# Eight of the sixteen transfers of turned blocks go from GpSimd's queue to ScalarE's

## The chip, the cores and the metric

The kernel runs on one core of one Trainium2 chip. A core has five engines with a queue of instructions each: PE (TensorE, matmuls), DVE (VectorE), ACT (ScalarE), POOL (GpSimd) and SP (SyncE). Each queue runs in order: an instruction that waits holds back everything behind it on its engine. DMA transfers are issued from the queues of SP, ACT and POOL and then run on 16 DMA engines that all the queues share. The metric is device time in microseconds, the median of several executions. The traces are of one profiled execution each.

## The reference

The input `x` has 8 images of 4096 tokens with 192 channels. A causal convolution with 7 taps comes first (softmax of `weight`, one set of taps for each of 8 heads of 24 channels), then a mixer over tokens, then one over channels:

```python
out = np.einsum('hk,bskhg->bshg', softmax(weight), x_unf)   # 7 taps, causal
xt = x.transpose(0, 2, 1)                                   # x is the result above
h = np.maximum(xt @ w_tok1, 0.0) @ w_tok2                   # 4096 -> 256 -> 4096
u = x + h.transpose(0, 2, 1)
h2 = np.maximum(u @ w_ch1, 0.0) @ w_ch2                     # 192 -> 1536 -> 192
return (u + h2).astype(np.float32)
```

## The kernel before

The images go in five groups: one, one, and three pairs. A group is computed in two stages. The first (convolution on ACT and DVE, lines 646 to 660, and the first token product on PE, lines 762 to 768) runs in the background, woven into the second stage of the group before it. The second stage takes 8 tiles of 512 tokens of the group. A tile goes through these steps:

- **mix2** (lines 921 to 950, or `mix2_halves`, lines 956 to 973, in the last two groups) is the second token product. DVE adds it to the convolved input, which gives `u` (tokens along the partitions), and turns `u` in blocks of 32 by 32 (`nc.vector.transpose`, lines 939, 950 and 973).
- **blocks_sent** (line 995) moves the turned blocks to their places, so that channels stand along the partitions. It is 16 DMA transfers of 48 KB each, all inside the core's SBUF. Until the last one has landed the tile can't be used.
- **parted** (line 1031; `parted_single` for a group of one image) splits the result into a high part (`own_hi`, ACT, line 1042 or 1021) and a low part (`own_lo`, DVE, line 1044 or 1027), and copies halves across partitions for the second image (ACT line 1047, POOL's queue line 1049).
- **channel1** (lines 1080 to 1122) multiplies by `w_ch1`, in six steps of two PSUM tiles. ACT takes the ReLU of each tile into `hh` (line 1121), DVE the rest into `hl` (line 1122), and only then is the PSUM tile free. The pool `ps_x` has six such tiles, so a step can begin when the step three before it has been read by both.
- **channel2** (lines 1156 to 1163, or `channel2_halves`, lines 1139 to 1147) multiplies by `w_ch2`, adds `u`, and stores to `out`.

The order of every queue is written out by the program before it runs (a planner, `Background`, places the background's steps by estimated times; it is not touched here). There are 27 calls of `blocks_sent`. The first three prepare tiles of a group of one image; the next 13 prepare pairs, with background work still running; the last 11 are in the stretch where no background is left. In those last 11, `blocks_sent` is called between the two images of a tile: behind channel1 of the first image and ahead of channel1 of the second. Below the calls are numbered 0 to 26 in order of time.

Each DMA takes one of 16 completion semaphores in turn: eight, named DMAHW0 to DMAHW7, serve the transfers of SP and ACT, and eight, DMASW0 to DMASW7, those of POOL. A transfer waits until the one that last used its semaphore has landed.

The background's split for the first token product is ACT's cast at line 746 (`xhl`, high part) and DVE's subtraction at line 750 (low part); PE's lines 766 to 768 read both.

Of the kernel before, what the change touches and what calls it, by code (L numbers as in the profile page):

```python
# [139 lines left out]
def conv_mixer_kernel(ctx: ExitStack, tc: tile.TileContext, x, weight, w_tok1, w_tok2, w_ch1, w_ch2, out):  # L140
    nc = tc.nc
# [25 lines left out]
    def f32(ap):  # L167
        return ap.bitcast(F32)
# [809 lines left out]
    def own_tile(n):  # L978
        return up.tile([P, ND, TT], F32R, name=f"own_{n}")
# [15 lines left out]
    def blocks_sent(z, nb, pool, name):  # L995

        if nb == 1:
            other = own_tile("lo")  # L1000
            blocks = z[:, :D // QB].rearrange("p (c n) t -> p n c t", n=NQ // 2)
            home = other
        else:
            other = pool.tile([P, 2, ND, TT], F32R, name=name)
            blocks = z.rearrange("p (c n) t -> p n c t", n=NQ)
            home = other[:, 1]
        for k in range(NQ):
            for q in range(NQ):
                i = (q + k) % NQ
                queue = nc.gpsimd if q % 2 else nc.sync  # L1010
                queue.dma_start(
                    out=f32(home[q * QB:(q + 1) * QB, :, i * P:(i + 1) * P]),
                    in_=blocks[i * QB:(i + 1) * QB, q % (2 * nb)],
                )
        return other
# [260 lines left out]
    for gi, bs in enumerate(GROUPS):  # L1276
# [13 lines left out]
        for q in range(NT):  # L1290
            nxt = (gi, q + 1) if q + 1 < NT else (gi + 1, 0)
            for i, b in enumerate(bs):
# [24 lines left out]
                if ready:  # L1317
                    abc = parted(other)
                elif turn:
                    if gi == 0 and nxt[0] == 0:  # L1320
                        bg.require(("t2", nxt[1] // 2, nxt[1] % 2))
                    z = up.tile([P, ND * NQ, P], F32, name="own_hi") if by_blocks else None
                    mix2(*nxt, *loaded, turned=z)
                    mixed[0] = nxt[1]
                    if by_blocks:
                        other = blocks_sent(z, len(GROUPS[nxt[0]]), sp, "other")
                        bg.release()
# [3 lines left out]
                if early:  # L1331
                    z = cps[0].tile([P, RB + HALO, 2, D // 2], F32, name="raw0")
                    z = z.rearrange("p r b d -> p (r b d)")[:, :ND * NQ * P].rearrange("p (n t) -> p n t", t=P)
                    for j in range(TJ):
                        mix2_halves(nxt[0], *loaded, z, j)
                        channel2_halves(i, h, u, osb, [j])
                    spare = not spare
                    other = blocks_sent(z, 2, cps[0] if spare else sp, "xc0" if spare else "other")
                elif ahead:
                    product2(i, h, u, osb, half[0])  # L1340
# [60 lines left out]
```

## Time and profile before

| What | Value |
|---|---|
| median of 3 runs | 2024.13 us (2024.07 to 2025.25) |
| the profiled execution | 2022.08 us |
| its span, first to last instruction | 2020.3 us |
| PE busy | 2010.3 us (100% of the span) |
| DVE busy | 1513.3 us (75%) |
| ACT busy | 756.7 us (37%) |
| POOL busy | 233.9 us (12%) |
| TensorE clock granted | 1.000 |

Views of the profile used below are the page of the profiled execution, the waits by engine, the busy time by windows, the view of one source line, and the timeline. In the timeline a row gives the start (us from the start of the span), the length (us), the engine, the line, the operation, what it writes and reads, and how many instructions were merged into the row. In brackets stands the idle time of the engine before it and what ended it. Engines named SPq or POOLq stand for their sequencers.

### The profile page before, as it was taken

The page shows a single profiled execution, that of the slowest core. Times are in us where ns is not written, and L with a number is a line of the kernel's source. Part 1 is how long each engine was busy: PE and PEld are TensorE (multiplying, and loading weights), DVE is VectorE, ACT ScalarE, POOL GpSimd, SP SyncE. Part 2 cuts the span into 40 slices and gives each one's busy share as a digit, 9 for nine tenths or more (in the row PEclk, how much of TensorE's full clock was granted, in tenths as well). Part 3 has the DMA queues.
Part 4 walks back from the last instruction along what each step waited for, and adds up shares of the span by engine and source line. Part 5 has one row for each costly group of instructions (what it writes and reads, how often), then busy time and mean ns, then how long its engine had stood idle before and what let it go on. Part 6 is the DMA issues. An engine that isn't in the chain of part 4 may idle for free.

```text
span 2020.3 us, 44927 instructions
## 1 busy us (share of the span) xinstructions
PE 2010.3 (100%) x18719; PEld 1860.6 (92%) x18719; DVE 1513.3 (75%) x3021; ACT 756.7 (37%) x1293; POOL 233.9 (12%) x407
## 2 busy tenths in 40 slices
PE   9999999999999999999999999999999999999999
PEld 9789999999999999999999999999999999999998
DVE  8799998999759999757975689556666666666664
ACT  4575544444333434324333334233233222333322
POOL 0100000101221011100111110111111110011110
PEclk9999999999999999999999999999999999999999
DMA  9845346456354577424654434533223222233310
GB/s 308 300 154 177 114 156 202 143 169 200 121 157 132 165 195 204 119 74 123 171 162 115 115 105 134 150 87 85 75 71 83 71 75 58 77 85 85 85 49 17
DMA packets 289626, 260.94 MB, mean 129 GB/s; under 512 B 205520, under 2 KB 238544, under 8 KB 289424
## 3 DMA queue, kind: packets, MB, share of 16 engines
q1 hardware_dynamic: 264736, 169.18, 29.6%
q0 software_dynamic: 24688, 88.89, 14.4%
q8 instruction: 148, 2.42, 0.5%
q14 instruction: 54, 0.44, 0.1%
HBM read 146.60 MB, written 71.30 MB: 108 GB/s over the span
## 4 chain that ended last, share of the span: by engine, by line
PE 95%; DVE 3%; ACT 1%; DMA 1%; issue 0%; POOL 0%; DVEq 0%; POOLq 0%; SPq 0%; ACTq 0%
PE ps_x L1080 38%; PE ps_x L1139 24%; PE ps_x L1156 13%; PE ps_x L1157 6%; PE ps_x L964 2%; PE ps_a L766 2%; PE ps_a L767 2%; PE ps_a L768 2%; PE ps_a L452 1%; PE ps_x L923 1%; PE ps_x L926 1%; PE ps_x L928 1%; PE ps_x L927 1%; DVE xc L659 1%; PE ps_a L762 1%; PE ps_x L989 1%
## 5 line engine op out<-in xcount | busy, mean ns | idle before, releaser
L1121 ACT ACTIVATE hh<-ps_x 128x512 fp32r<-128x512 f32 x756 | 410.7, 596 | 863.2 <-PE ps_x L1080 863.0
L1122 DVE SCALAR_TENSOR_TENSOR hl<-ps_x,hh 128x512 fp32r<-128x512 f32 x756 | 484.4, 685 | 184.1 <-ACT hh L1121 182.6
L1139 PE MATMUL ps_x<-w,hh 64*128 64x384 f32 x3360 | 481.5, 355 | 0.0
L1139 PE MATMUL ps_x<-w,hl 64*128 64x192 f32 x3360 | 423.0, 247 | 0.0
L659 DVE SCALAR_TENSOR_TENSOR xc<-raw,cw,xc 128x384 f32<-128x384 f32 (+1 forms) x768 | 389.0, 561 | 7.6 <-ACT xc L657 7.6
L1156 PE MATMUL ps_x<-w,hh 128*128 128x384 f32 x1344 | 387.2, 360 | 0.1
L1080 PE MATMUL ps_x<-other,w_hi 64*128 64x512 f32 x1296 | 336.8, 388 | 0.0
L1157 PE MATMUL ps_x<-w,hl 128*128 128x192 f32 x1344 | 336.4, 250 | 0.0
L1080 PE MATMUL ps_x<-own_hi,w_hi 64*128 64x512 f32 x1440 | 331.7, 392 | 1.6 <-DVE hl L1122 0.9
L1139 PEld LDWEIGHTS ps_x<-w,hl 64*128 64x128 f32 x3360 | 325.8, 188 | 1.2 <-DVE hl L1122 0.3
L1080 PE MATMUL ps_x<-own_lo,w_hi 64*128 64x512 f32 x1440 | 325.6, 387 | 0.0
L1080 PE MATMUL ps_x<-own_hi,w_lo 64*128 64x512 f32 x1440 | 325.6, 387 | 0.0
L1139 PEld LDWEIGHTS ps_x<-w,hh 64*128 64x128 f32 x3360 | 320.2, 184 | 0.9
L1157 PEld LDWEIGHTS ps_x<-w,hl 128*128 128x128 f32 x1344 | 256.6, 191 | 0.0
L1080 PEld LDWEIGHTS ps_x<-other,w_hi 64*128 64x128 f32 x1296 | 235.7, 184 | 21.6
L1156 PEld LDWEIGHTS ps_x<-w,hh 128*128 128x128 f32 x1344 | 252.4, 188 | 0.7 <-DVE hl L1122 0.7
L1080 PEld LDWEIGHTS ps_x<-own_hi,w_hi 64*128 64x128 f32 x1440 | 210.1, 184 | 34.3 <-issue 4.1
L1080 PEld LDWEIGHTS ps_x<-own_hi,w_lo 64*128 64x128 f32 x1440 | 215.6, 184 | 27.8 <-DVE w_lo L212 0.5
L1080 PEld LDWEIGHTS ps_x<-own_lo,w_hi 64*128 64x128 f32 x1440 | 215.9, 184 | 27.1
L1080 PE MATMUL ps_x<-other,w_lo 64*128 64x512 f32 x648 | 181.5, 386 | 0.0
L1147 DVE TENSOR_TENSOR osb<-ps_x,osb 128x192 f32<-128x192 f32 x420 | 150.2, 358 | 24.3
L1145 DVE TENSOR_TENSOR osb<-ps_x,u 128x192 f32<-128x192 f32 x140 | 49.8, 356 | 136.2 <-PE ps_x L1139 135.6
(165 smaller groups left out, 2443.3 us busy)
## 6 DMA issues: line engine op xcount, KB each, us to landing
raw<-in_x_dram SPq DMA_DIRECT2D x56, 672.0 KB, 7.3
t<-t2d SPq DMA_DIRECT2D x64, 512.0 KB, 5.5
out_dram<-osb POOLq DMA_DIRECT2D x63, 384.0 KB, 4.5
u<-xcd SPq DMA_DIRECT2D x62, 384.0 KB, 5.9
xcd<-xc POOLq DMA_DIRECT2D x28, 768.0 KB, 8.1
t<-t1p SPq DMA_DIRECT2D x32, 512.0 KB, 5.8
t2d<-stage SPq DMA_DIRECT2D x16, 512.0 KB, 3.7
t<-t1d SPq DMA_DIRECT2D x29, 256.0 KB, 5.2
```

The lines of the kernel that those rows point to most:

```text
L659: nc.vector.scalar_tensor_tensor(out=dst, in0=src, scalar=cw[:, h, k:k + 1], in1=dst, op0=ALU.mult, op1=ALU.add)
L766: nc.tensor.matmul(out=ps, lhsT=wh, rhs=xh, start=a, stop=False)
L767: nc.tensor.matmul(out=ps, lhsT=wh, rhs=xl, start=False, stop=False)
L768: nc.tensor.matmul(out=ps, lhsT=wl, rhs=xh, start=False, stop=z)
L1080: nc.tensor.matmul(out=ps, lhsT=w1[w][rows, c, p * P:(p + 1) * P], rhs=t[h][v][rows, c], start=n == 0, stop=n == len(prods) - 1,)
L1121: nc.scalar.activation(out=h["hh", f], in_=ps, func=AF.Relu)
L1122: nc.vector.scalar_tensor_tensor(out=h["hl", f], in0=ps, scalar=0.0, in1=f32(h["hh", f]), op0=ALU.max, op1=ALU.subtract)
L1139: nc.tensor.matmul(out=ps[:, :m], lhsT=h[part, f][ks, ts], rhs=w2[ks, f, :m], start=n == 0 and part == "hh", stop=z and part == "hl",)
L1145: nc.vector.tensor_tensor(out=rows(osb[:, j]), in0=rows(pss[0][:, :D]), in1=tokens(u, i)[:, j], op=ALU.add)
L1147: nc.vector.tensor_tensor(out=osb[:, j], in0=v, in1=osb[:, j], op=ALU.add)
L1156: nc.tensor.matmul(out=ps[:, :2 * D], lhsT=h["hh", f][:, ts], rhs=w2[:, f, :], start=n == 0, stop=False)
L1157: nc.tensor.matmul(out=ps[:, :D], lhsT=h["hl", f][:, ts], rhs=w2[:, f, :D], start=False, stop=z)
```

## The change

In `blocks_sent`, the transfers with odd `q` are put on ScalarE's queue where they were on GpSimd's. The other eight stay on SP's. Sizes, sources, destinations and the order in the program are the same.

```diff
@@ -1007,7 +1007,7 @@
         for k in range(NQ):
             for q in range(NQ):
                 i = (q + k) % NQ
-                queue = nc.gpsimd if q % 2 else nc.sync
+                queue = nc.scalar if q % 2 else nc.sync
                 queue.dma_start(
                     out=f32(home[q * QB:(q + 1) * QB, :, i * P:(i + 1) * P]),
                     in_=blocks[i * QB:(i + 1) * QB, q % (2 * nb)],
```

The order of PE and DVE is unchanged. ACT's queue gains 27 times eight transfers, and POOL's loses them.

The first place is ACT's queue in the last stretch, at call 17 (`raw_17298` is the buffer of turned blocks, `hh_17147` to `hh_17151` are outputs of channel1 for the first image, `hh_17601` and later for the second). Before:

```order
L1121 ACTIVATE hh_17149<-ps_x 128x512 [waits PE_49] x4
L1121 ACTIVATE hh_17151<-ps_x 128x512 [waits PE_49] x4
L1121 ACTIVATE hh_17601<-ps_x 128x512 [waits DVE_49,PE_49]
L1121 ACTIVATE hh_17601<-ps_x 128x512 [waits PE_49] x3
L1121 ACTIVATE hh_17603<-ps_x 128x512 [waits DVE_49,PE_49]
```

The same place in the changed kernel:

```order
L1121 ACTIVATE hh_17151<-ps_x 128x512 [waits PE_49] x4
L1011 DMA other<-raw_17298 32x3x128 [waits DMASW4_49,DVE_49]
L1011 DMA other<-raw_17298 32x3x128
L1011 DMA other<-raw_17298 32x3x128 [waits DMAHW6_49]
L1011 DMA other<-raw_17298 32x3x128 [waits DMAHW0_49]
L1011 DMA other<-raw_17298 32x3x128 [waits DMAHW2_49]
L1011 DMA other<-raw_17298 32x3x128 [waits DMAHW4_49]
L1011 DMA other<-raw_17298 32x3x128 [waits DMAHW6_49]
L1011 DMA other<-raw_17298 32x3x128 [waits DMAHW0_49]
L1121 ACTIVATE hh_17601<-ps_x 128x512 [waits PE_49,Activation_49]
```

The eight transfers stand between the ReLUs of the two images, and the first of them waits for DVE's last turn. The waits on DMAHW semaphores are new too: sixteen transfers share eight semaphores now and take them in turn, so SP and ACT have four each, and each of the last four here waits until the one four before it has landed.

The second place is ACT's queue at call 13, where the background's casts (`xhl`) and the first tap of the next convolution (line 657) follow:

```order
 L1121 ACTIVATE hh_14309<-ps_x 128x512 x4
 L1121 ACTIVATE hh_14311<-ps_x 128x512 x4
+L1011 DMA other<-own_hi 32x3x128 x8
 L746 CAST xhl<-xc_11786 128x768 x2
 L657 ACTIVATE xc_14648<-raw_14177,cw 128x16x24 x4
```

Both casts stand behind the transfers now.

The third is POOL's queue at the same call, where the store of a convolved block (`xcd`, line 694) follows:

```order
 L1170 DMA out_dram<-osb 128x768 x2
-L1011 DMA other<-own_hi 32x3x128 x8
 L694 DMA xcd_79<-xc_13815 128x8x192 x2
 L1049 DMA other<-own_hi 64x1536
 L1049 DMA other<-own_lo 64x1536
```

The store no longer has the transfers, and their wait for DVE, in front of it.

## The prediction

> **What bounds the kernel now.** I read the page first, then the busy time by windows, then PE's waits.
>
> ```profile
> PE 2010.3 (100%) x18719; PEld 1860.6 (92%) x18719; DVE 1513.3 (75%) x3021; ACT 756.7 (37%) x1293; POOL 233.9 (12%) x407
> PE 95%; DVE 3%; ACT 1%; DMA 1%; issue 0%; POOL 0%; DVEq 0%; POOLq 0%; SPq 0%; ACTq 0%
> ```
>
> PE is busy throughout and is 95% of the chain that ended last. The windows (columns: stretch, its length, then busy time and instructions of PE, PEld, DVE, ACT, POOL, the clock, DMA share, GB/s) say it stage by stage:
>
> ```profile
> 1080.00:1377.00 297.00, 297.00 (x2701) 275.75 (x2701) 204.47 (x393) 102.52 (x165) 33.72 (x59) 1.00 0.42 118
> 1377.00:1960.00 583.00, 583.00 (x6736) 538.37 (x6734) 366.11 (x740) 186.21 (x309) 71.83 (x131) 1.00 0.30 77
> ```
>
> In neither stretch does PE idle by 10 ns, and the granted clock is 1.00. Of PE's waits only one, of 1.4 us near the start, is longer than this one:
>
> ```profile
> PE ps_x L1080 <- DVE hl L1122: 0.9, 1, 0.9
> ```
>
> So nothing that makes the transfers land sooner can shorten these stretches: no wait of PE ends with them. The change can only cost time, and it does where ACT, which was free, is now held so long that PE has to wait for it. What counts is how long ACT is held, and how late it may be.
>
> **What it removes and adds.** The view of line 1011 gives the price of one issue (shortest, median, longest in ns); the last row is SP's timeline:
>
> ```profile
> L1011 SPq DMA_DIRECT2D other<-own_hi x104: 585/597/1542, 591.8 to 1335.8; - x104
> L1011 POOL DMA_DIRECT2D other<-own_hi x104: 548/548/582, 592.3 to 1337.3; - x104
> DMA to landing us min/median/max: 1.8/2.1/5.5
> ...
> 1263.21 0.33 SPq L724 DMA_DIRECT2D t<-t1p  x1
> ```
>
> POOL loses 27 x 8 x 548 ns = 118 us of work, which is worth nothing, since POOL is busy for 12% of the span. ACT gains 216 issues. No row shows a DMA issued by ACT. The nearest row is SP's, the same transfers from another engine that isn't POOL: 597 ns. Another transfer of SP's (line 724) was issued in 0.33 us, and the longest of line 1011 here took 1.54; these bound the price, and I take SP's own. Eight in a row are read from the timeline, at call 17, the second of the last stretch:
>
> ```profile
> 1432.56 0.58 DVE L973 STREAM_TRANSPOSE raw<-u 128x384 f32<-128x384 f32 x1
> 1433.27 5.10 SPq L1011 DMA_DIRECT2D other<-raw  x8
> 1436.34 1.09 ACT L1121 ACTIVATE hh<-ps_x 128x512 fp32r<-128x512 f32 x2 [18.87 <-PE ps_x L1080]
> 1436.97 1.29 DVE L1122 SCALAR_TENSOR_TENSOR hl<-ps_x,hh 128x512 fp32r<-128x512 f32 x2 [1.09 <-ACT hh L1121]
> 1440.22 0.39 PE L1080 MATMUL ps_x<-xc,w_hi 64*128 64x512 f32 x1
> ```
>
> **The last stretch, 11 calls.** ACT has been idle for 18.87 us when the second image's channel1 gives it its first ReLU at 1436.34. In the changed kernel its eight transfers start when SP's do, at 1433.27, behind DVE's last turn (1432.56 + 0.58 = 1433.14), and they stand ahead of that ReLU. ACT would be held until 1433.27 + 5.10 = 1438.37: the ReLU is 2.03 us late. Behind it wait `hl` on DVE and then PE, whose fourth step reuses the two PSUM tiles of the first. That step begins at 1440.22, and `hl` had read them by 1436.97 + 1.29 = 1438.26. The spare time is 1.96 us. So ACT may be held for 1436.34 - 1433.27 + 1.96 = 5.03 us from the start of its transfers; each us above that is a us of PE's. Later steps catch up, since ACT needs 1.09 and DVE 1.29 us of a step of about 2.04 us. The undisturbed eight thus cost 0.07 us a call. But not all were undisturbed:
>
> ```profile
> 1377.11 5.97 SPq L1011 DMA_DIRECT2D xc<-raw  x8
> 1657.48 5.83 SPq L1011 DMA_DIRECT2D other<-raw  x8
> 1713.54 5.65 SPq L1011 DMA_DIRECT2D xc<-raw  x8
> 1769.60 6.35 SPq L1011 DMA_DIRECT2D other<-raw  x8
> 1825.64 6.04 SPq L1011 DMA_DIRECT2D xc<-raw  x8
> ```
>
> These five of the eleven took 29.84 us in sum, 4.7 us above five times 5.03. I expect about as many disturbed calls after the change, not the same ones. The semaphores add little of their own: a queue has four, so its fifth transfer comes 4 x 5.10 / 8 = 2.55 us behind its first, and a landing takes 2.1; only slow landings hold the queue, and those are what stretched the five. Term: 4.7 + 6 x 0.07 = 5.1 us. At 0.33 us an issue it is nothing. At 0.75 us (8 x 0.75 = 6.0 us) it is 11 x 0.97 + 4.7 = 15.4 us.
>
> **The casts of the background, calls 5 to 8 and 12 to 15.** ACT had done both casts before the transfers began; now they come behind them. At call 13, and one call later for SP:
>
> ```profile
> 1198.48 0.84 ACT L746 CAST xhl<-xc 128x768 fp32r<-128x768 f32 x1 [2.28 <-PE ps_a L768]
> 1201.82 5.11 SPq L1011 DMA_DIRECT2D other<-own_hi  x8
> 1204.62 0.95 DVE L750 TENSOR_TENSOR xhl<-xc,xhl 128x768 fp32r<-128x768 f32 x1
> 1209.44 0.36 PE L766 MATMUL ps_a<-xhl,t 128*128 128x384 f32 x1
> 1266.55 5.63 SPq L1011 DMA_DIRECT2D other<-own_hi  x8
> ```
>
> From the start of the transfers to PE's first use are 1209.44 - 1201.82 = 7.62 us. A cast (0.84) and a subtraction (0.95) have to follow the transfers, so ACT may be held 5.83 us, some 5.7 with a hand-over between engines (ACT's first ReLU above ended at 1436.34 + 0.60 and DVE started at 1436.97, so 0.03 to 0.05 each). Undisturbed, 0.6 us is left; at call 14, with 5.63, hardly any. What is late next is DVE's work behind line 750, by about 3.5 us, which the idle time on DVE (25% of the span) takes up before the next channel1.
>
> Two of these calls, 7 and 13, get a store in their way:
>
> ```profile
> 1194.96 1.14 DVE L659 SCALAR_TENSOR_TENSOR xc<-raw,cw,xc 128x384 f32<-128x384 f32 x2
> 1202.48 4.36 POOL L1011 DMA_DIRECT2D other<-own_hi  x8 [19.05 <-DMA t<-t1p]
> 1206.83 1.82 POOL L694 DMA_DIRECT2D xcd<-xc  x2
> xcd<-xc POOLq DMA_DIRECT2D x28, 768.0 KB, 8.1
> ```
>
> The convolved block was done at 1194.96 + 1.14 = 1196.10, yet its store (two DMAs, 8.1 us to landing) went behind POOL's transfers at 1206.83. Now it can go at 1196.1, and its second half is still moving when the sixteen transfers start at 1201.82. I price this by the five stretched rows: 0.5 to 1.2 us longer than 5.1, so 0 to 0.5 us over what is left, and take 0.5 us for each of the two. Below it is nothing; above, if each of the two waves of landings took the 5.5 us of the slowest in place of 2.1, some 6 us a call. Term: 1.0 us.
>
> **The other calls, 0 to 4 and 9 to 11.** At call 0 casts and a first tap move behind the transfers too, and the split starts about 1.3 us later. PE's need is here:
>
> ```profile
> 494.92 1.89 DVE L1027 TENSOR_TENSOR own_lo<-own_lo,own_hi 128x512 fp32r<-128x512 f32 x3 [0.75 <-ACT own_hi L1021]
> 498.21 0.50 PE L1080 MATMUL ps_x<-own_hi,w_hi 64*128 64x512 f32 x2
> ```
>
> DVE was done at 496.81, PE began at 498.21, and the low part is used last in a step, so the 1.40 us and more cover it. Without that cover it would be some tenths of a us a call. I cost these calls at nothing.
>
> **The sum.** 5.1 + 1.0 = 6.1 us on the profiled execution of 2022.08 us (its span is 2020.3, so 1.8 us lie around it): 2028.2. The median shown is 2024.13, which is 2.05 us above the profiled execution; with that the forecast is 2030.2, rounded 2030 us.
>
> **Rivals.** (a) *Not slower.* ACT's hold stays under 5.03 us and PE notices nothing. It speaks for it that six of the eleven rows are only 0.07 us above that point, and that POOL needed 4.36 us for the same eight. With POOL's pace the undisturbed calls cost nothing and the five stretched ones, each 0.74 us shorter, 1.2 us in all; the casts have 1.4 us to spare. Time: 2024.13 + 1.2 = 2025.3, which counts as no change. Against it stands that SP, the nearer row, shows no issue under 585 ns. [...]
>
> (b) *ACT issues more dearly than SP,* because its sequencer is slower at it, or because two queues that issue at once share what makes the descriptors. The trace shows SP and POOL side by side, never two queues of this kind, so it can't exclude it; that single issues of SP stretched to 1.54 us says that an issue can be held by something else. At 0.75 us: 15.4 + about 3 for the casts = 18 us, 2042. At twice SP's price, eight take 10.2 us: 11 x 5.2 + 6 x 4.5 + 2 x 3.4 = 91 us, 2115; calls 5 and 6 have a PE use about 1.1 us later. [...]
>
> (c) *Faster:* a POOL that is free earlier, or transfers that land sooner. PE's 583.00 busy us of 583.00 leave no room for either. Time: 2024.
>
> (d) *The change doesn't do what it says:* the order shows it 27 times on ACT, so no chance is kept for it.
>
> **How the numbers follow.** Forecast 0.50, (a) 0.28, (b) 0.19, (c) 0.03. About 0.2%, 4 us, is what a measurement of this kernel can tell from no change. Slower by more than that: 0.50 + 0.19 = 0.69; the same 0.28; faster 0.03. The range goes from 2023, nothing lost and 1 us for the spread of the runs, to 2048: (b) at 0.8 us an issue, 6.4 us held, is 11 x 1.37 + 4.7 + 8 x 0.5 = 24 us. The doubled price lies outside.
>
> **What would show it.** ACT's rows of line 1011 at about 600 ns, eight in 5.1 to 6.4 us. In the last stretch the first ReLU behind them 2 to 3.3 us later, and PE waiting for `hl` of line 1122 at the fourth step of channel1, 0 to 1.3 us a call, some 5 us in all. At the calls with casts, line 750 late by about 4 us and PE's wait at line 766 under 1 us. POOL's `xcd` stores at calls 7 and 13 about 8 to 10 us earlier. I am wrong if an issue on ACT is far from 0.6 us, if PE waits in the last stretch for something other than `hl`, or if most of the loss lies before 1377 us.

## The result: 35 us slower, and the profile after

| | before | changed |
|---|---|---|
| median of 4 runs each | 2024.38 us (2024.07 to 2025.25) | 2059.05 us (2055.71 to 2060.12) |
| ratio | | 1.0168 (95% interval 1.0150 to 1.0185) |
| the profiled execution, its span | 2022.08 us, 2020.3 us | 2057.99 us, 2056.0 us |

The sign is as forecast, the size is not: 35 us where 6 were predicted, outside the range of 2023 to 2048. Engines and chain of the changed kernel, from its page:

```profile
PE 2029.0 (99%) x18719; PEld 1869.5 (91%) x18719; DVE 1508.8 (73%) x3021; ACT 753.7 (37%) x1293; POOL 114.5 (6%) x191
PE 77%; DVE 13%; DMA 3%; ACTq 3%; ACT 2%; issue 1%; SPq 0%; DVEq 0%; POOL 0%; POOLq 0%
```

PE had 95% of the chain and has 77% now; DVE, ACT's sequencer and DMA have the rest. PE's three longest waits (total us, times, longest):

```profile
PE ps_x L1080 <- DVE hl L1122: 8.6, 8, 1.5
PE ps_a L766 <- ACT xhl L746: 4.6, 3, 2.0
PE ps_a L767 <- DVE xhl L750: 1.5, 3, 0.6
```

The view of line 1011 gives the price of one issue on ACT (shortest, median, longest in ns) and the landings:

```profile
L1011 ACTq DMA_DIRECT2D other<-own_hi x104: 592/612/2013, 593.7 to 1355.0; - x104
...
L1011 ACTq DMA_DIRECT2D other<-raw x40: 592/620/1712, 1454.4 to 1919.7; - x40
...
DMA to landing us min/median/max: 1.9/2.0/6.4
```

The waits are the predicted ones: `hl` in the last stretch, the casts at lines 766 and 767 before it. The issue price is the predicted one too, 612 to 620 ns. To see where the time went, compare the intervals between the starts of the calls. For the ten intervals of the last stretch the windows are, before and after (length, then busy PE, PEld, DVE, ACT, POOL):

```profile
1377.11:1937.76 560.65, 560.65 (x6486) 518.14 (x6484) 352.19 (x712) 175.30 (x292) 65.83 (x120) 1.00 0.30 77
```

```profile
1396.27:1971.44 575.17, 568.25 (x6484) 524.37 (x6482) 349.41 (x712) 173.22 (x292) 21.94 (x40) 1.00 0.29 75
```

The same matmuls take 14.5 us longer; the eleventh call adds 2.0 us behind the last of these starts (2056.0 - 1971.44 = 84.6 us to the end, 82.5 before). The other 19.2 us (1396.27 - 1377.11) arose before call 16. So the loss is in two halves of 16.5 and 19.2 us.

**The last stretch.** Some of ACT's eleven batches, from its timeline, then call 17 on each engine:

```profile
1396.27 7.04 ACTq L1011 DMA_DIRECT2D xc<-raw  x8
1454.44 7.29 ACTq L1011 DMA_DIRECT2D other<-raw  x8
...
1685.15 5.66 ACTq L1011 DMA_DIRECT2D other<-raw  x8
...
1971.44 6.72 ACTq L1011 DMA_DIRECT2D xc<-raw  x8
...
1457.45 0.55 POOL L1170 DMA_DIRECT2D out_dram<-osb  x1 [29.59 <-DVE osb L1147]
1461.83 3.05 ACT L1121 ACTIVATE hh<-ps_x 128x512 fp32r<-128x512 f32 x6 [23.24 <-DMA other<-raw]
1462.46 3.68 DVE L1122 SCALAR_TENSOR_TENSOR hl<-ps_x,hh 128x512 fp32r<-128x512 f32 x6 [5.32 <-ACT hh L1121]
1463.21 0.50 PE L1080 MATMUL ps_x<-xc,w_hi 64*128 64x512 f32 x1 [1.48 <-DVE hl L1122]
```

The chain of call 17 reads as predicted: eight transfers, then the ReLU, then `hl`, then PE. But all eleven batches are stretched, to 5.66 to 7.29 us, 70.5 us in sum, where the forecast had five stretched and 60.4 in sum. New is the POOL row. Before the change the same store of the output stood behind POOL's transfers:

```profile
1433.78 4.36 POOL L1011 DMA_DIRECT2D other<-raw  x8 [27.18 <-DVE raw L973]
1438.13 0.59 POOL L1170 DMA_DIRECT2D out_dram<-osb  x1
```

That is 4.86 us after the start of call 17 at 1433.27, when SP's eight were nearly issued. Now it goes 3.01 us after the start at 1454.44, in the middle of the batch, and in all eleven calls alike. The store isn't all of it, though: in call 17 an issue of ACT that began before the store took 1.71 us instead of 0.61. What else stretches batches stands in the section on the stores that are held back.

```profile
1456.40 1.71 ACTq L1011 DMA_DIRECT2D other<-raw  x1
```

Issues like this one are most of the stretch. An undisturbed batch takes 5.16 us (eight issues of 0.61 and seven gaps of 0.04). What the eleven batches take beyond that is 13.7 us: 12.8 lie in single issues of 0.7 to 1.9 us, and only 0.9 in longer gaps, where the waits for the landing of the transfer four before would show. SP's disturbed batches before the change are alike, with one long issue each (1.16 to 1.86 us) and no such gap. At call 23 before:

```profile
1771.52 1.86 SPq L1011 DMA_DIRECT2D other<-raw  x1
```

**The first part.** Six of its intervals hold the whole loss: behind call 0 (32.55 us before, 36.27 now), 5 (64.72, 66.96), 6 (66.09, 68.00), 7 (63.53, 67.73), 13 (64.73, 68.79) and 14 (64.73, 68.49), 19.9 us in sum; the others, each between -1.2 and +1.4 us, cancel. They are of two kinds. At 7, 13 and 14 POOL's store of the convolved block went ahead. Call 7 in the timeline:

```profile
842.08 1.79 POOL L694 DMA_DIRECT2D xcd<-xc  x2 [16.14 <-DVE xc L659]
845.01 8.80 ACTq L1011 DMA_DIRECT2D other<-own_hi  x8
853.86 1.56 ACT L746 CAST xhl<-xc 128x768 fp32r<-128x768 f32 x2 [18.94 <-DMA other<-own_hi]
854.72 0.96 DVE L750 TENSOR_TENSOR xhl<-xc,xhl 128x768 fp32r<-128x768 f32 x1 [7.99 <-ACT xhl L746]
```

And the windows of 3.41 us around the end of PE's wait (length, busy PE, PEld, DVE, ACT, POOL, then the clock, DMA share and GB/s):

```profile
851.49:854.90 3.41, 1.44 (x11) 1.21 (x9) 0.18 (x1) 1.04 (x2) 0.00 (x0) 1.00 0.46 109
854.90:858.31 3.41, 2.99 (x9) 2.60 (x10) 3.38 (x6) 3.16 (x5) 0.55 (x1) 0.50 0.04 8
```

ACT was held 8.80 us (8.33 and 8.12 in calls 13 and 14). In these three calls the waits for landings do hold the queue: the fifth transfer begins 0.9, 2.1 and 1.0 us late, right when the first has landed; the rest is in long issues. Behind PE's wait came 3.41 us at a granted clock of 0.50: PE's matmuls of lines 766 to 768 start 0.32 us apart there, and 0.17 us right behind it. PE was busy for 2.99 us of it, so that about 1.5 us were lost, by my estimate. Half clock followed calls 13 and 14 too, with PE busy for 3.41 and 3.27 us, about 1.7 and 1.6 us lost. At 0, 5 and 6 the batch is ordinary or a little stretched (5.59, 6.65, 5.18 us), but DVE has no idle time left. Behind call 5 it is busy for all of the 12 us from 734.00, behind call 6 for 9.96 of the 10 us from 793.00. Call 0 in the timeline:

```profile
486.49 5.59 ACTq L1011 DMA_DIRECT2D own_lo<-own_hi  x8
492.18 0.62 ACT L730 CAST t<-t 128x512 fp32r<-128x512 f32 x1 [13.77 <-DMA own_lo<-own_hi]
492.83 0.69 DVE L734 TENSOR_TENSOR t<-t 128x512 fp32r<-128x512 f32 x1 [4.68 <-ACT t L730]
```

And what follows it by windows:

```profile
498.20:510.00 11.80, 11.23 (x85) 8.00 (x83) 11.73 (x24) 4.55 (x9) 1.09 (x2) 1.00 0.36 114
```

DVE waits 4.68 us for ACT's cast of `t`, which stands behind the transfers now, and is then busy for 11.73 of 11.80 us. It can't make up what it lost, and PE pays.

### The profile page after: what moved, and what is told of

Its sections match the earlier page's. It is cut to its first block, busy times and chain, and to the rows that moved or that the text cites. A ratio compares the mean times of both kernels' runs of the same rounds, so it can differ in the third digit from the quotient of the medians.

```text
span 2056.0 us, 44524 instructions
## 1 busy us (share of the span) xinstructions
PE 2029.0 (99%) x18719; PEld 1869.5 (91%) x18719; DVE 1508.8 (73%) x3021; ACT 753.7 (37%) x1293; POOL 114.5 (6%) x191
## 3 DMA queue, kind: packets, MB, share of 16 engines
q8 instruction: 148, 2.42, 0.5%
## 4 chain that ended last, share of the span: by engine, by line
PE 77%; DVE 13%; DMA 3%; ACTq 3%; ACT 2%; issue 1%; SPq 0%; DVEq 0%; POOL 0%; POOLq 0%
PE ps_x L1080 30%; PE ps_x L1139 19%; PE ps_x L1156 10%; PE ps_x L1157 4%; DVE xc L659 4%; DVE hl L1122 3%; ACTq L1011 3%; PE ps_x L964 2%; PE ps_a L767 1%; PE ps_a L768 1%; PE ps_a L766 1%; DMA other<-own_hi 1%; DVE osb L1147 1%; PE ps_a L452 1%; PE ps_x L923 1%
## 5 line engine op out<-in xcount | busy, mean ns | idle before, releaser
L1139 PE MATMUL ps_x<-w,hh 64*128 64x384 f32 x3360 | 493.9, 355 | 0.0
L1139 PE MATMUL ps_x<-w,hl 64*128 64x192 f32 x3360 | 473.8, 247 | 0.0
L1139 PEld LDWEIGHTS ps_x<-w,hl 64*128 64x128 f32 x3360 | 392.7, 188 | 0.5
L1139 PEld LDWEIGHTS ps_x<-w,hh 64*128 64x128 f32 x3360 | 391.3, 184 | 0.8
L1080 PE MATMUL ps_x<-other,w_hi 64*128 64x512 f32 x1296 | 341.4, 390 | 5.4 <-DVE hl L1122 4.4
L1080 PE MATMUL ps_x<-own_hi,w_hi 64*128 64x512 f32 x1440 | 336.6, 395 | 4.6 <-DVE hl L1122 2.1
```

Of the source, the lines that this page charges most:

```text
L1080: nc.tensor.matmul(out=ps, lhsT=w1[w][rows, c, p * P:(p + 1) * P], rhs=t[h][v][rows, c], start=n == 0, stop=n == len(prods) - 1,)
L1139: nc.tensor.matmul(out=ps[:, :m], lhsT=h[part, f][ks, ts], rhs=w2[ks, f, :m], start=n == 0 and part == "hh", stop=z and part == "hl",)
```

## Theories

Theory 1, formed from this: ACT's hold is what costs, 1 us for each us above 5.03 in the last stretch, and the hold grew because POOL's stores, no longer queued behind POOL's transfers, collide with the batch. The rivals: two queues that issue side by side and share eight semaphores slow each other by themselves; slow landings cost by themselves, whoever issues; the loss is spread over all calls rather than bound to places.

The experiments, e1 to e12, were run in three groups, each beside the kernel before on the same chip (medians 2023.3, 2022.0 and 2023.1 us in the three). "Ratio" is always to that.

## Experiment: four transfers on ACT instead of eight

```diff
-                queue = nc.scalar if q % 2 else nc.sync
+                queue = (nc.sync, nc.scalar, nc.sync, nc.gpsimd)[q]
```

> Of the eight transfers on ScalarE's queue four go back to GpSimd's (q = 3), and SP keeps eight. Theory 1 (the price is what ScalarE is held above 5.03 us in a call): ScalarE is held about 2.5 us, at most 4 with slow landings, under the 5.03 us, so that the last stretch loses nothing and the casts come 1.9 us earlier than they are needed: 2024 to 2030, mid 2026. Theory 2 (any use of ScalarE's queue next to SP's costs, by contention on the way): about half of the loss of 35 us stays, near 2041.

e2: 2024.37 us, ratio 1.0008 (0.9998 to 1.0017). The ten intervals of the last stretch by windows:

```profile
1379.13:1939.66 560.53, 560.53 (x6484) 518.02 (x6482) 350.88 (x712) 175.28 (x292) 44.20 (x80) 1.00 0.29 77
```

Two of ACT's batches in the timeline, a usual one and the longest:

```profile
1771.50 2.56 ACTq L1011 DMA_DIRECT2D other<-raw  x4
1827.56 4.00 ACTq L1011 DMA_DIRECT2D xc<-raw  x4
```

PE is busy for every one of the 560.53 us. The batch of 4.00 us is stretched (its last issue took 2.04 us, beside landings of 4 to 5 us), as those of the changed kernel are, and costs nothing, because it ends before 5.03 us. So it is the hold, with its threshold, and not the use of ACT's queue as such.

## Experiment: the last eleven calls alone, and the first sixteen alone

`calls` is a list that grows by one with each call of `blocks_sent`, here and in the experiments below.

```diff
-                queue = nc.scalar if q % 2 else nc.sync
+                odd = nc.scalar if len(calls) > 16 else nc.gpsimd      # e3; e4 with the two exchanged
+                queue = odd if q % 2 else nc.sync
```

> ScalarE's queue is used in the last eleven calls only; the first sixteen use GpSimd's, as before. Theory 1 (the loss of each call stands for itself): the eleven intervals lose 14 to 15 us and the tail 2, so 2024.4 + 16.6 = 2041 (2038 to 2044). Theory 2 (the last stretch inherits lateness from the first, in ScalarE's or DVE's queue): clearly less than 16 us, under 2035.

> The other half of the test: ScalarE's queue in the first sixteen calls only, GpSimd's in the last eleven. Theory 1: 2024.4 + 19 = 2043.5 (2040 to 2047), with the half clock behind calls 7, 13 and 14, and the two halves add to the 35 us of the whole. Theory 2 (the halves interact): the sum of the two losses is over 5 us off 35.

e3: 2036.98 us, ratio 1.0069 (1.0054 to 1.0084). e4: 2039.74 us, ratio 1.0075 (1.0058 to 1.0092). By the ratios that is 14.0 and 15.2 us, 29 in sum, against 34 for the whole, at the edge of the 5 us that theory 2 was given; the profiled executions add up better (14.1 and 19.1 of 35.7 us of span). Both are somewhat under what was expected, and e4's runs spread over 4.7 us. The traces show that the last stretch doesn't inherit its loss: in e4, which lost 19 us ahead of it, the ten intervals take 560.64 us, against 560.65 before the change, and in e3 they lose 13.1 us with nothing lost ahead of them.

## Experiment: transfers in the last eleven calls issued between the ReLUs

```diff
+                if q % 2 and len(calls) > 16:
+                    behind.append(send)
+                else:
+                    send()
...
+            for send in [behind.pop(0) for _ in behind[:2 if p < 2 else 1]]:
+                send()
```

> GpSimd's queue in the first sixteen calls; in the last eleven ScalarE issues its eight transfers behind the ReLUs of the six steps of channel1 (two, two, one, one, one, one), so that no ReLU stands behind more than two. Theory 1 (only the hold of ScalarE's queue costs): two issues hold ScalarE 1.2 us, less than the 5.03 us less what a step needs, and the transfers have 30 us until they are needed: 2024 to 2027. Theory 2 (the queue or its traffic costs, wherever the transfers stand): as e3_last11, 2035 or more.

e7: 2023.30 us, ratio 1.0003 (0.9993 to 1.0012). The same eight transfers from the same queue in the same eleven calls, with POOL's stores as free as in e3, cost 14 us in e3 and nothing here. Where they stand in ACT's queue is what counts.

## Experiment: all sixteen on SP

```diff
-                queue = nc.scalar if q % 2 else nc.sync
+                queue = nc.sync
```

> All sixteen transfers on SP, in about 10.5 us; ScalarE has none, and GpSimd's stores are as free as in the changed kernel. Theory 1 (the collision costs only through ScalarE's hold): the last eleven intervals stay at 56.05 us in spite of slow landings, since the moved tile is needed some 30 us later; the calls of the background lose where the landing is late (some 5 us later than before): 2024 to 2035. Theory 2 (slow landings cost by themselves): the last eleven intervals are over 56.5 us as well, 2040 or more.

e8: 2084.87 us, ratio 1.0304 (1.0289 to 1.0319): the total is a miss by 50 us, the part on the last stretch a hit. One batch in SP's timeline:

```profile
1664.94 10.67 SPq L1011 DMA_DIRECT2D xc<-raw  x16
```

The ten intervals by windows:

```profile
1440.62:2001.26 560.64, 560.64 (x6486) 518.13 (x6484) 351.23 (x712) 175.17 (x292) 21.87 (x40) 1.00 0.29 77
```

With POOL's stores free and landings of 3 to 4.6 us among the batches, PE still loses nothing in the last stretch, so slow landings alone do no harm there. In the first sixteen calls the landing, 5 us later, is itself on the path; 63.5 us had been lost by call 16. PE's waits there are for the split of the moved tile:

```profile
PE ps_x L1080 <- ACT other L1047: 11.1, 6, 2.0
PE ps_x L1080 <- ACT own_hi L1021: 7.0, 2, 5.3
```

Theory 1 had taken the background calls to have that much time to spare. They haven't.

## Experiment: POOL's stores held back again

A small read of every moved block on POOL, behind each call, so that no store can start before the transfers have landed. The first version had its scratch in a new tile of 16 bytes a partition, the second in a tile that is dead by then.

```diff
+    gate = const.tile([P, TT // P], F32, name="gate")                                  # e1 only
...
+        nc.gpsimd.tensor_copy(out=gate, in_=f32(home[:, 0, 0:TT:P]))                   # e1
+        nc.gpsimd.tensor_copy(out=csm[:, 0:TT // P], in_=f32(home[:, 0, 0:TT:P]))      # e5
```

> ScalarE keeps its eight transfers. GpSimd reads a column of every moved block behind each call, so that its stores (of the convolved block, line 694, and of the output, line 1170) can't start before the transfers have landed. Theory 1 (GpSimd's stores, freed by the change, collide with the batch): ScalarE's batches fall from a mean of 6.4 us in the last eleven calls to about 5.5; the three batches of 8.7 to 9.1 us (calls 7, 13, 14) fall under 6.5; no stretch of half clock behind them; the eleven intervals lose 8 to 10 us in all over the kernel before, where the changed kernel loses 14.5; total 2036 to 2046, mid 2041. Theory 2 (two queues of the same kind that issue side by side and share eight completion semaphores slow each other, whatever GpSimd does): batches stay at 5.7 to 7.3 us and the time at 2055 or more.

e1: 2058.97 us, ratio 1.0177 (1.0162 to 1.0193): by the total, theory 2. But the trace showed short batches, 5.16 to 5.36 us, in five of the last eleven calls and in calls 13 and 14, and no stretch of half clock; the time was lost elsewhere, in slower matmuls. Hence the second version:

> The same gate on GpSimd, but its scratch is the dead tile csm, so that no buffer moves in SBUF. In e1_gate the batches were short as theory 1 said (5.16 to 5.19 us in calls 13, 14, 19 to 21 and 23, no half clock), yet the matmuls of channel1 came every 0.233 us in place of 0.227 us, from before the first gated call on. Theory 1 (moved buffers made those matmuls slower and hid the gain): pitch 0.227 us again; what is left is some 9 us in the last eleven calls, from batches that other traffic stretches, and some 10 us in the first sixteen, where only calls 7, 13 and 14 gain: 2042 (2036 to 2046). Theory 2 (the gate itself slows the matmuls, or holding back the stores doesn't help): 2055 or more.

e5: 2042.16 us, ratio 1.0099 (1.0084 to 1.0114), as expected. The ten intervals by windows:

```profile
1386.81:1956.17 569.36, 565.90 (x6484) 521.97 (x6482) 349.32 (x712) 173.22 (x292) 23.77 (x50) 1.00 0.29 75
```

ACT's batch and POOL's store at call 20 in the timeline:

```profile
1615.66 5.18 ACTq L1011 DMA_DIRECT2D xc<-raw  x8
...
1623.33 0.55 POOL L1171 DMA_DIRECT2D out_dram<-osb  x1 [0.36 <-issue]
```

The store comes 7.67 us after the call's start, and the batch is back at 5.18 us. The last stretch's ten intervals lose 8.7 us instead of 14.5; the three behind calls 7, 13 and 14 lose 0.7 us in sum instead of 12.0, and the clock stays at 1.00. So the freed stores made about 17 of the 35 us by these intervals, and 15.6 by the spans (2056.0 less 2040.4), since other intervals came out longer in this execution. The rest is ACT's hold without them.

Five of the eleven batches here are at 5.2 to 5.3 us and six at 6.1 to 6.7. What sets the six apart stands in the view of the DMA queues (queue, kind: packets, MB, share of the 16 engines). These two rows are in the view of call 17's batch (6.72 us) and not in that of call 20's (5.18 us):

```profile
q8 instruction: 1, 0.02, 1.6%
q14 instruction: 1, 0.01, 0.4%
```

A 16 KB packet of queue q8, of the kind "instruction", starts inside each of the six long batches and inside none of the five short ones. In the kernel before it is the same: the five disturbed batches of SP in the last stretch (5.65 to 6.35 us) each hold such a packet, the six others (5.09 to 5.11 us) none. In the changed kernel the seven batches that hold one take 5.93 to 7.29 us, the four without 5.66 to 5.89. So two kinds of traffic stretch the batches: these packets, which were there before the change, and the freed stores, which came on top. That the packets are a cause is read from the coincidence alone; no run varies them.

## Experiment: SP's eight to GpSimd, ACT keeps its own

```diff
-                queue = nc.scalar if q % 2 else nc.sync
+                queue = nc.scalar if q % 2 else nc.gpsimd
```

> ScalarE keeps its eight transfers; SP's eight go to GpSimd. ScalarE's queue then has no second queue of its kind beside it and all eight of its semaphores, and GpSimd's stores stand behind eight transfers again. Theory 1 (stores and shared semaphores stretch the batch): no transfer of ScalarE's waits for a landing, the batch is 8 x 0.59 = 4.7 to 5.0 us even where landings are slow, under the 5.03 us, so that the last eleven calls lose nothing (0 to 3 us) and calls 7, 13 and 14 nothing; calls 0, 5 and 6 keep some 6 us: 2028 to 2036, mid 2031. Theory 2 (ScalarE's issue itself is what costs): batches over 5.5 us and 2045 or more.

e6: 2042.80 us, ratio 1.0104 (1.0087 to 1.0121): between the two theories, 12 us above the middle of theory 1. ACT's issue price with no second queue of its kind beside it:

```profile
L1011 ACTq DMA_DIRECT2D other<-own_hi x104: 592/611/1626, 594.2 to 1346.0; - x104
```

SP's load at call 18, whose transfers start at 1501.07 here, and then the same place in the kernel before:

```profile
1498.85 1.94 SPq L873 DMA_DIRECT2D t<-t2d  x2
```

```profile
1489.33 5.11 SPq L1011 DMA_DIRECT2D xc<-raw  x8
1494.54 1.06 SPq L873 DMA_DIRECT2D t<-t2d  x2
```

Two things follow. The price is 611 ns here and 612 ns in the changed kernel, so SP's issues beside them don't make ACT's dearer (SP's own median there is 612 ns too, against 597 before): the "dearer issue" rival is out, and my 4.7 to 5.0 us for eight was too low (5.15 at best). And the queue that was relieved is SP's now, and its next load goes ahead of the batch, as POOL's store did: at call 18 ACT's eighth transfer is held for 0.74 us by the semaphore of this load, which lands at 1506.36, and the batch takes 5.91 us. That explains one call. Six of the others in the last eleven are stretched (5.5 to 6.3 us) by single long issues, 0.95 to 1.76 us, with no wait for a landing, and each of these six holds a 16 KB packet of the kind "instruction". So theory 1 was wrong that a batch with semaphores enough can't be stretched.

## Experiment: which of the first sixteen calls cost

The edit is against e4.

```diff
-                odd = nc.gpsimd if len(calls) > 16 else nc.scalar
+                odd = nc.gpsimd if len(calls) > 16 or len(calls) in (1, 6, 7, 8, 14, 15) else nc.scalar
```

> As e4_first16, but calls 0, 5, 6, 7, 13 and 14 keep GpSimd's queue; ScalarE's has the other ten of the first sixteen. Theory 1 (the loss of the first part lies in these six calls: in three the convolved block's store collides and the half clock follows, in three DVE had no idle time behind ScalarE's late cast): 2024 to 2028, no half clock. Theory 2 (each call of the background costs about 1.2 us, and more shows up at some calls only because lateness adds up): ten sixteenths of e4_first16's 15 to 19 us, 2034 or more.

e9: 2026.68 us, ratio 1.0016 (1.0007 to 1.0026): by the ratios 3.2 us of e4's 15.2 are left, with no half clock. Ten calls out of sixteen cost that much together; the six make the rest. The split within the six is less sure: in the profiled execution the interval behind call 6 is 3.9 us longer than before (69.94 against 66.09), although ACT had none of its transfers; GpSimd's own landed late there (up to 5.0 us, 2.5 before).

## Experiment: twelve on ACT

The edit is against e3.

```diff
-                queue = odd if q % 2 else nc.sync
+                queue = odd if q % 2 or (q == 0 and len(calls) > 16) else nc.sync
```

> As e3_last11, but twelve of the sixteen transfers are ScalarE's in the last eleven calls, four SP's. Theory 1 (a us of PE for each us that ScalarE is held above 5.03 us): twelve issues of 0.65 us are 7.8 us, with some stretching 8.0 to 8.4, so 3.0 to 3.5 us a call: 2057 to 2064; and if PE's idle time of 2.5 us and more trips the half clock, as behind calls 7, 13 and 14, 1.7 us a call on top, up to 2080. Theory 2 (transfers that land late cost, and fewer on SP's queue change nothing in that): as e3_last11, near 2038.

e10: 2088.07 us, ratio 1.0324 (1.0308 to 1.0339), above the upper end, since the batches took 7.9 to 9.8 us rather than 8.0 to 8.4. Call 17 in ACT's timeline:

```profile
1443.56 8.71 ACTq L1015 DMA_DIRECT2D other<-raw  x12
```

By windows, its interval to the next call, and the two windows of 3.41 us ahead of and in the half clock:

```profile
1443.56:1505.03 61.47, 58.48 (x652) 54.05 (x650) 34.82 (x71) 17.23 (x29) 2.20 (x4) 0.97 0.27 70
1451.78:1455.19 3.41, 1.34 (x9) 0.90 (x11) 2.19 (x4) 2.81 (x6) 0.00 (x0) 1.00 0.56 147
1455.19:1458.60 3.41, 3.41 (x20) 2.67 (x18) 1.99 (x4) 1.32 (x3) 0.00 (x0) 0.50 0.00 0
```

With the measured batch the rule holds again: 8.71 - 5.03 = 3.68, and half a clock for 3.41 us is 1.7, together 5.38; the interval is 5.42 us above 56.05. Over the kernels:

| kernel, call | ACT held, us | above 5.03 | interval less 56.05 |
|---|---|---|---|
| four on ACT, 24 | 4.00 | 0 | 0.00 |
| stores held back, 20 | 5.18 | 0.15 | 0.28 |
| changed, 21 | 5.66 | 0.63 | 0.74 |
| changed, 17 | 7.29 | 2.26 | 2.42 |
| last eleven only, 25 | 7.37 | 2.34 | 2.45 |
| twelve on ACT, 21 | 9.27 | 4.24 | 5.97, of which 1.7 at half clock |

## Experiment: does the place of the buffers cost?

This settles what went wrong in e1. The kernel before, with an unused tile:

```diff
     ident = const.tile([P, P], F32, name="ident")
+    pad = const.tile([P, 4], F32, name="pad")       # e12: [P, 64]
+    nc.gpsimd.memset(pad, 0.0)
```

> The kernel before, with an unused tile of 16 bytes a partition placed behind ident, where e1_gate had its scratch; all later buffers move by as much, and nothing else changes but one memset. Theory 1 (the place of the buffers made e1_gate's channel1 slower): matmuls of channel1 at 0.233 us in place of 0.227 us, 2040 to 2046. Theory 2 (the gate's own work did it): 2022 to 2026.

> The same with an unused tile of 256 bytes a partition. If what counts is that the buffers start on a multiple of some tens of bytes: no change, 2022 to 2026. If it is any move, or the free room that the kernel has at the top: as e11_pad16, 2040 or more.

e11: 2045.34 us, ratio 1.0110 (1.0095 to 1.0125). e12: 2023.38 us, ratio 1.0001 (0.9992 to 1.0010). Matmuls of channel1 in 560 us of the last stretch (busy PE and their number stand behind the length), in e11, then in e12:

```profile
1390.00:1950.00 560.00, 255.62 (x2160) 200.66 (x2160) 1.00 0.30 77
```

```profile
1377.00:1937.00 560.00, 248.60 (x2160) 200.81 (x2160) 1.00 0.30 77
```

The same 2160 matmuls take 2.8% longer with all buffers 16 bytes further, and no longer than before with 256. For the kernel's 6912 matmuls of channel1 that makes 7.0 x 6912 / 2160 = 22 us; 22 were measured.

## Why the prediction was wrong

- *PE is the bound, nothing can be gained:* right. No variant is faster than the kernel before.
- *An issue on ACT costs SP's 0.597 us:* right, 0.612 to 0.620, with or without SP beside it. The rivals of a dearer issue and of a doubled price are refuted by e6; what two queues might share as they issue was my supposition, and no run shows it. ACT at POOL's pace, the "not slower" rival, is refuted by the same row. Eight in a row hold the engine for 5.2 us at best, against a landing of 2.0 us (median).
- *5.03 us of hold in the last stretch, then 1 us of PE per us:* right, but for 0.12 us: 39 of forty batches of four kernels (the changed one, e3, e5, e6) cost 0.10 to 0.16 us more than the rule gives, one 0.42, so the time to spare is nearer 4.9 us. The rule tells beforehand that four on ACT cost nothing.
- *The length of the batch, "about as many disturbed calls after the change", 5.1 us in all:* **this term failed.** All eleven were stretched, 70.5 us in sum instead of 60.4, and the loss is 16.5 us. Of the 11.4 us that the term lacked, about 6.1 are the freed stores, 3.9 longer batches without them (64.3 us in sum with the stores held back) and 1.4 the 0.12 us of each call. I had looked at what the relieved POOL would do only for line 694 in two calls. The output's store at line 1170 stood behind POOL's transfers in every one of the last eleven, in the very order that I read, and I didn't ask where it would go. With the stores held back the ten intervals lose 8.7 instead of 14.5 us. The count of calls that other traffic disturbs was near: six batches hold a packet of the kind "instruction" with the stores held back, seven in the changed kernel, five before.
- *The semaphores: "only slow landings hold the queue, and those are what stretched the five":* wrong. The five were single long issues without a wait for a landing, and so is most of the stretch after the change; waits for landings hold ACT's queue by up to 2.1 us in calls 7, 13 and 14, and by 0.4 us at most in the last eleven.
- *The store of the convolved block costs 0.5 us in each of calls 7 and 13, 1.0 us:* the mechanism was right, the size wrong, and a call was overlooked. Calls 7, 13 and 14 cost 12.0 us. My own upper bound (each wave of landings at the slowest landing, some 6 us a call) was nearer to the 4 us than the value I took. About 1.5 to 1.7 us of each is the half clock, which no row of before could show and which I didn't reckon with.
- *Calls 0 to 4 and 9 to 11 at nothing, and DVE's lateness taken up by its idle 25%:* **failed at calls 0, 5 and 6**, 7.9 us. The cover at call 0 was read from the split alone (1.40 us), not from DVE's whole queue. The kernel before's own window shows what I didn't look up, DVE busy for 11.67 of the 11.80 us in which it would have had to catch up:

```profile
498.20:510.00 11.80, 11.80 (x103) 9.94 (x104) 11.67 (x22) 5.33 (x10) 1.09 (x2) 1.00 0.36 113
```

An idle share of 25% over the whole span says nothing about these 12 us.
- *"I am wrong if most of the loss lies before 1377 us":* it does, 19.2 of 35.7 us.
- A slip in rival (a): the five stretched rows at POOL's pace come to 1.1 us above 5.03, not 1.2. Nothing rests on it.

## What to carry to other kernels

When a queue is relieved of work, ask what stood behind that work: it can go earlier (POOL's output store at call 17 went 3.01 us after the call's start instead of 4.86), and if it is a transfer, into the very batch that was moved. Price the move on the receiving queue by the time until its next needed instruction, stage by stage, with the idle time of the engines behind it read in the window in question and not over the span. If the work has slack, put it between the needed instructions in portions smaller than the spare time: the same eight issues cost 14 us in one block (e3) and nothing in pieces (e7).

## What the runs showed of the hardware that was not expected

**Half clock after a partly idle window.** In the changed kernel the granted clock fell to 0.50 three times inside the span, at 854.90, 1223.54 and 1291.80 us, for 3.41 us each. These starts are 368.64 and 68.26 us apart, about 108 and 20 times that length, so I count windows of 3.41 us from there. The three windows ahead of the half ones had PE busy for 1.44, 1.42 and 1.77 us; the emptiest one that had no half one behind it had 2.07:

```profile
1220.13:1223.54 3.41, 1.42 (x8) 0.94 (x7) 1.20 (x2) 1.56 (x2) 0.00 (x0) 1.00 0.60 133
1288.39:1291.80 3.41, 1.77 (x11) 1.29 (x9) 0.87 (x1) 1.57 (x2) 0.00 (x0) 1.00 0.45 106
731.96:735.37 3.41, 2.07 (x15) 1.17 (x14) 3.41 (x8) 3.41 (x7) 0.00 (x0) 1.00 1.04 363
```

In the changed kernel 1.6 to 2.0 us of idle time inside one window thus went ahead of a half one. The other runs show no sharp border: windows at full clock with PE busy for up to 1.94 us (a share of 0.57, in e4) were followed by a half one, while one of 1.68 us (0.49, in e9) and one of 1.84 us (0.54, in e8) were not; from 2.02 us (0.59, in e6) on none was. A window that itself ran at half clock was followed by another one after shares of up to 0.75 (e10).

**Sixteen bytes of SBUF.** Moving the buffers by 16 bytes a partition (e11) made the matmuls of channel1 2.8% slower and the kernel 1.1%; with 256 bytes (e12) both stayed as before, the kernel at a ratio of 1.0001. An experiment that adds a tile may measure this, as e1 did, if the other buffers don't stay where they are.

**An interval that isn't constant.** From call 3 to 4 the profiled executions took 56.4 us (before) to 57.8 us (e7 and e10, which are the same kernel up to call 15). One execution's interval in the first part is good to about 1.4 us, not better.
